# Linear attention and a SwiGLU gate on one core: every PSUM-fed query evacuation split between ScalarE and VectorE, and both denominator runs placed in gate/up

## The chip, the cores and the metric

The kernel runs on one core of a Trainium2 chip. The metric is the device time of one execution in microseconds (us); the time given for the kernel before is the median of three runs. TensorE is PE in the profile (its weight loads PEld), VectorE is DVE, ScalarE is ACT, GpSimd is POOL, and SyncE (SP) issues all DMAs.

## The reference

The inputs are bf16: x is 1 x 2048 x 1024, wqkv 1024 x 3072, wo 1024 x 1024, w_gate and w_up 1024 x 3584, w_down 3584 x 1024. A second x among the inputs is not used.

```python
def A(xn):                                     # linear attention, 32 heads of 32
    q, k, v = split(xn @ wqkv)
    phi = lambda t: where(t > 0, t + 1, exp(t)) + 1e-6
    pq, pk = phi(q), phi(k)
    kv  = einsum("bhsd,bhse->bhde", pk, v)
    z   = einsum("bhsd->bhd", pk)
    num = einsum("bhqd,bhde->bhqe", pq, kv)
    den = einsum("bhqd,bhd->bhq", pq, z)[..., None] + 1e-6
    return heads_together(num / den) @ wo
def B(xn):
    return (silu(xn @ w_gate) * (xn @ w_up)) @ w_down
xn = layernorm(x)
out = x + A(xn) * silu(B(xn))
```

## The kernel before, in words

All large products but the smallest are Strassen-Winograd products of seven multiplications (called m = 1 to 7), and some of the seven (those in a set J) are split into seven again. One such product is a *pair*: two weight blocks (w = 0, 1) against one token half of 1024 tokens (p = 0, 1). A result of 2 x 2 blocks comes out of PSUM by the callback `evac(w, i, j, ...)`, where i is the column block and j the token block. Three of the four results are read from a PSUM bank (`kind == "ps"`: from m = 2, m = 3 and m = 4), the fourth from an SBUF tile (`"sb"`, m = 7). In each pair m = 6 and m = 7 go on in the same banks, and DVE adds drain them (`step(w, m)`); a split product has four steps (`fresh(m, k)`), whose sums also run on DVE and ACT.

The stages are, in this order: layer norm, transposition and the keys and values (kv); four *query pairs* `q_pair(p, s)`, with s the half of the columns; 28 gate/up pairs `gu_pair(p, n)`; four pairs for s = (normalised queries) @ M, where M combines kv and wo; and the down projection with the final sum. Among the queries the sixteen blocks of M are made as well (`m_build`, each a small product, an ACT evacuation and a DMA store to `m_scratch`).

- `phi_evac` computes phi of a drained block. ACT makes Exp; DVE takes min(e, 1) + 1e-6 (the tensor_scalar in line 1041). Then one of two forms follows. With `relu` false, a DVE scalar_tensor_tensor makes max(t, 0) + e (line 1048) and reads t from its source, a PSUM bank where kind is "ps". With `relu` true, ACT makes Relu(t) into an SBUF tile of the pool H1 and DVE adds two SBUF tiles (line 485). `RQ` chooses the form for the queries, `RK` for the keys.
- `den_run(s)` makes the denominators of half s from the finished queries of both token halves: 32 small matmuls with Zh into one bank, one DVE tensor_scalar (line 1296), four DVE reciprocals (line 1298), an ACT copy, and eight DMAs into `r_scratch`.
- `normalise(p, j, half)` reads `r_scratch` back, scales the rows on ACT and multiplies the queries on DVE, then stores them in `q_scratch`. Eight such calls stand behind gate/up pairs z = 4, 6, ..., 18 (`N0`, `NS`); the first four are half 0.
- The sums of weights that Strassen needs (`combos`) and the sums for the split products (`inner`) run on POOL for gate/up, except the combos of its first weight block, which run on DVE.

Nothing of the order is written out by hand below the level of these calls. `Plan.op` records every operation with its reads and writes, `Plan.schedule` gives each a due time from what depends on it, and then chooses, for all engines together, the operation that can start first by its own costs; banks and buffers are given out there as well. The chosen order is what each engine runs, with semaphores between engines. So moving one call can move operations of others on every engine. Operations of DVE that read SBUF alone are marked `port`, and the planner starts them only when POOL's current operation is over by its own costs; on the chip nothing but the semaphores orders POOL against DVE.

The lines of the profile for all these are helpers: 427 for matmuls, 456 for transposes, 477 for ACT, 485 for tensor_tensor on DVE and POOL, 497 for DMAs.

## Time and profile before

| what | value |
|---|---|
| median of 3 runs | 730.34 us (730.07 to 732.97) |
| the profiled execution | 730.07 us |
| its span | 728.3 us |
| mean granted TensorE clock | 0.997 |
| PE busy | 707.5 us |
| DVE busy | 548.0 us |
| ACT busy | 365.1 us |
| POOL busy | 283.5 us |
| first denominator run, PE | at 155.22 us |
| second denominator run, PE | at 208.33 us |
| reads of `r_scratch` | 225.6 to 388.4 us |

The span is what the profile covers; the execution's own time is 1.8 us longer. The groups of the profile are named by line, engine, operation and operands; as most lines are those of helpers, an instruction is told apart by its operands (`ps` is PSUM, `SB` the large SBUF tile) and by its place in the order.

### The profile page before, as it was taken

To read this page: it belongs to the slowest core of one execution; us is meant where nothing else is said; L and a number is where in the kernel's file an instruction comes from. 1 tells how busy PE (TensorE), PEld (TensorE's weight loads), DVE (VectorE), ACT (ScalarE), POOL (GpSimd) and SP (SyncE) were. 2 spreads that over 40 slices of the span, in tenths; PEclk is the share of its full clock that TensorE was granted. 3 is DMA by queue.
4 is the path that set the end of the run, shared out by engine and by line. 5 is a ranking of instruction groups with operands and counts; after the bars stand their busy time and mean duration, and the time that the engine had idled before them with its cause. 6 is when DMAs were issued, how large, how long until landed. Compare 5 with 4: busy or idle time off the path is not lost.

```text
span 728.3 us, 11805 instructions
## 1 busy us (share of the span) xinstructions
PE 707.5 (97%) x4247; PEld 401.0 (55%) x4247; DVE 548.0 (75%) x1099; ACT 365.1 (50%) x713; POOL 283.5 (39%) x258
## 2 busy tenths in 40 slices
PE   8999999988999999999999999999999999999997
PEld 3444545544666666666666666566454455464643
DVE  6998766989997787777777777789699875555433
ACT  3777745876646556665665545445573112121212
POOL 2011000255667966788676877433640000000000
PEclk9999999999999999999999999999999999999999
DMA  9334244230234244533445824254798356473622
GB/s 297 108 82 108 45 115 147 86 119 6 84 99 131 103 150 148 167 112 121 141 156 165 264 85 137 67 167 148 255 300 259 91 157 202 132 206 90 187 73 72
DMA packets 141979, 101.58 MB, mean 139 GB/s; under 512 B 19040, under 2 KB 137056, under 8 KB 141920
## 3 DMA queue, kind: packets, MB, share of 16 engines
q1 hardware_dynamic: 141920, 100.82, 45.8%
q8 instruction: 33, 0.54, 0.3%
q14 instruction: 26, 0.21, 0.1%
HBM read 68.16 MB, written 29.49 MB: 134 GB/s over the span
## 4 chain that ended last, share of the span: by engine, by line
PE 81%; DVE 7%; DMA 7%; ACT 3%; issue 1%; SPq 0%; POOL 0%; DVEq 0%; ACTq 0%
PE ps L427 81%; DVE SB L485 3%; ACT SB L477 2%; DMA out_dram<-SB 1%; DVE SB L1041 1%; DMA SB<-q_scratch 1%; DMA SB<-in_A_x_dram 1%; DMA SB<-SB 1%; DVE SB L1048 1%; DMA SB<-h_scratch 1%; DMA SB<-in_A_wqkv_dram 1%; DVE ps L485 1%; ACT ps L477 1%; SPq L497 0%; DVE SB L1213 0%
## 5 line engine op out<-in xcount | busy, mean ns | idle before, releaser
L427 PE MATMUL ps<-SB 128*128 128x512 f16 (+4 forms) x4126 | 697.2, 331 | 12.5 <-ACT ps L477 3.3
L427 PEld LDWEIGHTS ps<-SB 128*128 128x128 f16 (+1 forms) x4126 | 395.1, 98 | 312.2 <-DVE ps L485 8.3
L485 POOL TENSOR_TENSOR SB<-SB 128x512 f16<-128x512 f16 (+5 forms) x224 | 269.4, 1238 | 190.6 <-DMA SB<-in_B_w_up_dram 75.6
L477 ACT ACTIVATE SB<-ps 128x512 f16<-128x512 f32 (+4 forms) x427 | 225.6, 559 | 178.5 <-PE ps L427 164.5
L485 DVE TENSOR_TENSOR SB<-ps,SB 128x256 f32<-128x256 f32 (+2 forms) x318 | 182.0, 592 | 71.7 <-PE ps L427 56.3
L485 DVE TENSOR_TENSOR SB<-SB 128x512 f16<-128x512 f16 (+9 forms) x316 | 184.6, 618 | 59.3 <-ACT SB L477 21.7
L485 DVE TENSOR_TENSOR ps<-ps,SB 128x512 f32<-128x512 f32 (+1 forms) x250 | 128.3, 527 | 30.3 <-PE ps L427 25.2
L477 ACT ACTIVATE ps<-ps 128x512 f32<-128x512 f32 (+1 forms) x172 | 84.2, 491 | 97.4 <-PE ps L427 93.9
L477 ACT ACTIVATE SB<-SB 128x512 f16<-128x512 f32 (+1 forms) x68 | 42.1, 620 | 78.0 <-DVE SB L485 77.5
L1005 POOL TENSOR_TENSOR rstd<-veps,neg_half 128x1 f32<-128x1 f32 x16 | 11.4, 724 | 64.2 <-DVE veps L1004 62.9
L1041 DVE TENSOR_SCALAR SB<-SB 128x512 f16<-128x512 f16 x64 | 22.7, 367 | 8.7 <-ACT SB L477 8.7
L477 ACT ACTIVATE SB<-SB,zc 128x512 bf16<-128x512 bf16 x32 | 21.9, 710 | 2.5 <-DVE SB L485 2.5
L1048 DVE SCALAR_TENSOR_TENSOR SB<-ps,SB 128x512 bf16<-128x512 f32 x25 | 16.6, 678 | 0.1
L477 ACT ACTIVATE SB<-SB,nmr,rstd 128x1024 f16<-128x1024 bf16 x12 | 14.6, 1236 | 1.2 <-DVE nmr L1007 1.1
L1001 DVE BATCH_NORM_STATS2 stats<-SB 128x6 f32<-128x512 bf16 x16 | 10.9, 683 | 3.4 <-DMA SB<-in_A_x_dram 3.4
L1048 DVE SCALAR_TENSOR_TENSOR SB<-SB 128x512 bf16<-128x512 f32 x15 | 11.3, 756 | 0.0
L1002 DVE BATCH_NORM_STATS2 stats<-SB 128x6 f32<-128x512 bf16 x16 | 10.8, 678 | 0.0
L427 PE MATMUL ps<-SB,ident 128*128 128x512 f16 x17 | 6.5, 555 | 1.4 <-POOL ident L508 1.4
L456 PE MATMUL ps<-ident,SB 128*128 128x128 f16 x40 | 3.1, 222 | 1.6 <-DVE SB L1213 1.0
L456 PEld LDWEIGHTS ps<-ident,SB 128*128 128x128 f16 x40 | 2.5, 99 | 3.9 <-DVE SB L1011 1.9
L427 PEld LDWEIGHTS ps<-SB,ident 128*128 128x128 f16 x17 | 2.1, 128 | 4.6 <-issue 2.8
L1298 DVE RECIPROCAL SB<-SB 128x64 f32<-128x64 f32 x8 | 4.4, 547 | 0.1
(28 smaller groups left out, 23.3 us busy)
## 6 DMA issues: line engine op xcount, KB each, us to landing
h_scratch<-SB SPq DMA_DIRECT2D x112, 128.0 KB, 2.9
SB<-h_scratch SPq DMA_DIRECT2D x16, 896.0 KB, 6.2
SB<-in_B_w_gate_dram SPq DMA_DIRECT2D x14, 512.0 KB, 4.2
SB<-in_B_w_up_dram SPq DMA_DIRECT2D x14, 512.0 KB, 5.4
SB<-in_B_w_down_dram SPq DMA_DIRECT2D x4, 1792.0 KB, 7.8
SB<-in_A_wqkv_dram SPq DMA_DIRECT2D x12, 512.0 KB, 7.0
SB<-in_A_x_dram SPq DMA_DIRECT2D x16, 256.0 KB, 3.1
SB<-r_scratch SPq DMA_DIRECT2D x32, 128.0 KB, 2.8
```

The lines of the kernel that those rows point to most:

```text
L427: last = h.matmul(o() if callable(o) else o, l() if callable(l) else l, r() if callable(r) else r, start=st, stop=sp, skip_group_check=True)
L456: last = h.transpose(o(), i(), ident[:, :])
L477: return op("act", reads, writes, lambda h: h.activation(ev(o), ev(i), func, **kw), n / 1200.0 + (0.055 if src == "ps" else 0.095) + (0.09 ...
L485: f = lambda h: h.tensor_tensor(ev(o), ev(a), ev(b), alu)
L1001: dve([xr] + ([named("ve", 0)] if q == 1 else []), [sA], lambda h: h.bn_stats(stats[:, j, 0, :], xa[:, 0:512]), 512)
L1002: dve([xr] + ([named("ve", 0)] if q == 1 else []), [sB], lambda h: h.bn_stats(stats[:, j, 1, :], xa[:, 512:1024]), 512)
L1005: pool([ver, nh_r], [rsr], lambda h: h.tensor_tensor(rstd[:, j, :], veps[:, j, :], neg_half[:, :], ALU.pow), 0.56)
L1041: dve([e], [e], lambda h: h.tensor_scalar(vap(e, FP16), vap(e, FP16), 1.0, EPS_PHI, ALU.min, ALU.add), 512, 3.84, urgent=PU).port = True
L1048: dve(reads + [e], [out_r], lambda h: h.scalar_tensor_tensor(out_ap, ev(src), 0.0, vap(e, FP16), ALU.max, ALU.add), 512, urgent=PU).port = ...
L1298: dve([ea], [ra], lambda h, q=q: h.reciprocal(vap(ra, F32)[:, q * 64:q * 64 + 64], vap(ea, F32)[:, q * 64:q * 64 + 64]), 400)
```

## The change

There are two parts. `RQ` becomes true for every query block that comes from PSUM, where it was true only for those with j = 1; so the blocks from m = 2 and m = 4 also take the form with Relu on ACT and an add on DVE. And the two calls of `den_run` move: the first from between the third and the fourth query pair to the third gate/up pair (z = 2), the second from z = 2 to z = 6. `ZD` is then no longer read.

```diff
     UBANK, PU = 0.0, 6.0
-    RQ = lambda w, i, j, kind: kind == "ps" and j == 1
+    RQ = lambda w, i, j, kind: kind == "ps"
     RK = lambda q, c, kind: c == 0
...
         q_pair(0, 1, Q[1], mix=mb[6:])
-        den_run(0)
         G[0] = gu_load(0)
         G[0].inner(IE, JG)
         q_pair(1, 1, Q[1])
...
             at = []
-            if z == ZD:
-                at.append(partial(den_run, 1))
+            if z in (2, 6):
+                at.append(partial(den_run, z // 6))
             gu_pair(p, n, G[n], at)
```

The function that `RQ` steers:

```python
def phi_evac(reads, src, kind, out_ap, out_r, relu=False):
    e = tmp(H1)
    act(reads, [e], partial(vap, e, FP16), src, ACT.Exp, 512, kind)
    dve([e], [e], ...min(e, 1.0) + EPS_PHI...)
    if relu:
        r = tmp(H1)
        act(reads, [r], partial(vap, r, FP16), src, ACT.Relu, 512, kind)
        tt([e, r], [out_r], ...e + r...)
        return
    dve(reads + [e], [out_r], ...max(src, 0.0) + e...)
```

In the emitted order of the changed kernel the rest moves as follows. On SP the loads of the second gate/up weights (block n = 1) come after fourteen of the sixteen block stores (before, the gate half came after ten and the up half after twelve), and the eight stores to `r_scratch` of the first run come among the h_scratch stores of gate/up. On DVE, ahead of the drain of step (w0, m7) of the last query pair stand two line-1041 instructions and two SBUF adds of `phi_evac` (before: the first denominator run's five instructions, one drain and two line-1041 instructions); seven drains from PSUM follow in a row, then eight instructions that read SBUF alone, the drain of (w0, m6) of the first gate/up pair's stretch, six more that read SBUF alone, and the drain (m5, k1). Late in gate/up the orders of the engines agree again.

## The prediction

> **What bounds the kernel now.** I read the page first, then the busy time by stretches, then PE's waits in the stretch that the change touches, then the chain and the timeline there.

> ```profile
> PE 707.5 (97%) x4247; PEld 401.0 (55%) x4247; DVE 548.0 (75%) x1099; ACT 365.1 (50%) x713; POOL 283.5 (39%) x258
> ```
> TensorE is busy for 97% of the 728.3 us span, so only its idle time and slow clock can be won. By stretches (columns: width, then busy us and instructions of PE, PEld, DVE, ACT, POOL, then granted clock, DMA share, GB/s):

> ```profile
> 124.00:153.00 29.00, 27.31 (x170) 15.25 (x168) 28.07 (x75) 23.89 (x51) 6.66 (x7) 1.00 0.33 105
> 153.00:161.00 8.00, 7.61 (x71) 4.43 (x72) 5.86 (x11) 5.09 (x12) 5.11 (x4) 1.00 0.61 187
> 161.00:182.00 21.00, 16.52 (x84) 8.34 (x83) 19.36 (x35) 12.12 (x25) 12.73 (x11) 0.92 0.02 6
> 190.00:440.00 250.00, 249.97 (x1638) 157.54 (x1637) 196.23 (x390) 143.30 (x294) 192.81 (x154) 1.00 0.43 137
> ```
> The queries (124 to 182) leave PE idle for 1.69 + 0.39 + 4.48 = 6.6 us, and 161 to 182 has a clock of 0.92. Gate/up (190 to 440) leaves 0.03 us idle. So the prize lies among the queries, and whatever moves into gate/up costs its PE time and nothing else, as long as DVE (196 of 250 us), ACT (143) and POOL (193) keep their slack. PE's waits from 124 to 190, and the timeline around the longest:

> ```profile
> PE ps L427 <- DVE SB L485: 2.9, 1, 2.9
> PE ps L427 <- DVE SB L1048: 1.1, 1, 1.1
> PE ps L427 <- DVE ps L485: 0.4, 1, 0.4
> ```
> ```profile
> 157.37 8.52 POOL L485 TENSOR_TENSOR SB<-SB 128x1024 f16<-128x1024 bf16 x4 [2.81 <-DMA SB<-in_B_w_up_dram]
> ...
> 159.80 4.04 DVE L1041 TENSOR_SCALAR SB<-SB 128x512 f16<-128x512 f16 x2
> ...
> 163.76 0.68 DVE L485 TENSOR_TENSOR SB<-ps,SB 128x512 f32<-128x512 f32 x1
> ...
> 164.49 1.03 PE L427 MATMUL ps<-SB 128*128 128x512 f16 x2 [2.91 <-DVE SB L485]
> ```
> Two L1041, usually 0.28 us each, take 4.04 us while POOL builds the combinations of the second gate/up weights, 2.13 us each (8.52 / 4). They do no more work; they wait for POOL. Behind them on DVE's queue stands the add that drains step (w0, m7) of the last query pair, and PE waits 2.91 us for it. After that PE runs 164.49 to 167.7 at half clock (the record has 3.41 us at 0.5, hence 0.92), which loses another 1.71 us. This one event costs 4.62 us.

> **The first part: sixteen evacuations.** Each query pair has four products with j = 0 drained from PSUM (m = 2 and m = 4, for w = 0 and 1); four pairs make 16. Removed are 16 L1048 with PSUM source, 0.60 us from start to start (two take 1.27). Added are 16 ACT Relu, at 0.50 (eight such evacuations take 4.03), and 16 DVE adds between SBUF tiles at 0.34 (0.41 alone, two take 0.75). DVE is relieved of 16 x 0.26 = 4.2 us, ACT gets 8.0 more.

> ```profile
> L1048 DVE SCALAR_TENSOR_TENSOR SB<-ps,SB x25: 642/677/692, 23.4 to 189.9; 128x512 bf16<-128x512 f32 x25
> L1048 DVE SCALAR_TENSOR_TENSOR SB<-SB x15: 678/681/1151, 36.2 to 194.9; 128x512 bf16<-128x512 f32 x15
> ```
> The PSUM form never exceeds 0.69 us; the form with both inputs in SBUF reaches 1.15, when POOL is at work (174.94, 175.94). An SBUF add also took 1.07 at 170.92 beside POOL's 1.14. So the new add is cheaper alone and dearer under POOL. [...]

> On ACT: from 130.91 to 153.34 it runs 45 instructions up to the copy (w0) that PE waits 0.71 us for at 153.39. In the changed order 48 stand there: four Relus and one block evacuation more, others fewer. 3 x 0.50 = 1.5 us, less the idle 0.92 at 144.70 and 0.2 at 149.06: PE goes on **0.4 us later**. If nothing absorbs it, 1.5; if earlier free banks absorb all, 0.

> **The second part: the denominators.** The first run takes from the queries 32 matmuls (1.06 us of PE), on DVE 0.42 + 2.31 us and 1.10 of idle before, on ACT 0.42, and on SP eight issues in 5.21 us.

> ```profile
> 155.22 1.06 PE L427 MATMUL ps<-SB,Zh 128*32 128x256 bf16 x32
> ...
> 156.79 2.31 DVE L1298 RECIPROCAL SB<-SB 128x64 f32<-128x64 f32 x4
> ```
> The PE time comes back whole in gate/up: net 0. There the second run stands today (PE at 208.33) without a wait of PE; the first takes that place, and the second goes four pairs on, to about 208.3 + 4 x 11.6 = 255 (eight normalisations start from 225.6 to 388.4, two pairs apart: 23.3 us per two pairs). The readers keep their places: the first half's at 225.6 stays 17 us behind, the second's at 225.6 + 4 x 23.3 = 319 is 64 us behind; a landing takes 2.8 us. On SP the eight issues no longer stand before the third gate/up weights, but among h_scratch stores; POOL has none of it. All of this I cost at 0, hidden by DVE's 54 idle us in 250; without that cover it would be its 2.7 us of DVE per run.

> **What happens at the stall.** In the changed order, four SBUF-only instructions (two L1041, two adds) stand ahead of the drain of (w0, m7), and then come seven PSUM drains in a row. PE reaches that pair at about 153.4 + 0.4; its inputs come over ACT at 0.5 us each, so the four end at about 157.3. POOL's first combination began at 157.37, after weights issued at 152.05; in the changed order those follow two to four more block stores, so not earlier. On these numbers the stall goes: **-4.6 us**. The margin is only some tenths.

> What is late next: after the seven drains come eight SBUF-only instructions (among them the adds put off), then the drain of gate/up's first (w0, m6), then six more, then the drain (m5, k1). They begin at about 164.0, with POOL in its last combination and the eight smaller inner sums still to come:

> ```profile
> 157.37 9.75 POOL L485 TENSOR_TENSOR SB<-SB 128x1024 f16<-128x1024 bf16 x5 [2.81 <-DMA SB<-in_B_w_up_dram]
> 169.77 6.77 POOL L485 TENSOR_TENSOR SB<-SB 128x256 f16<-128x256 bf16 x7 [2.65 <-PE ps L427]
> ```
> If each waits out one POOL instruction, as at 159.80 and 170.92 to 173.82, eight take 2.13 + 1.2 (9.75 - 8.52) + 6/7 x 6.77 = 9.1 us: the first drain ends at 164.0 + 9.1 + 0.7 = 173.8. PE needs it for the product (w0, m7), which it begins today at about 177.4 (its drain starts at 178.48); less 2.91, 1.71, 1.06 of waits and 1.06 of matmuls that left, plus 0.4, it is there at 171.1. It waits 2.7, then 0.9 for its product (174.7), and for the second drain (one POOL instruction 1.0, three L1041 at 0.2, two adds at 0.34, itself 0.4: 176.5) another 1.8. **New waits: 4.5 us.** Below, 0, where POOL is through early or the two alternate better; above, 8, if ACT's longer queue delays the cluster too. I take 4.5, as the rows for it are of the same instructions. The waits of 1.06 and 0.44 at 175.08 and 181.35 lie where these come, and go: **-1.5**.

> Clock: in this trace 2.91 us of idle led to half speed, 1.06 did not. 2.7 in one piece is nearer to the first, so 1.7 may be added. [...] I leave the 1.7 out of the point and keep it in the range.

> **Sum.** -4.6 - 1.5 + 0.4 + 4.5 = -1.2 us. The profiled execution took 730.07 us (span 728.3 and 1.8 around it; 0.27 below the median of 730.34): **728.9 us**. With the ends of the terms its own range is 724 (no new waits, nothing lost on ACT: -6.1) to 731.7 (1.1 more on ACT, the clock falls once).

> **Rivals.** (1) *The cluster does not bind*: the SBUF instructions slip between POOL's, or PE has other products to do, so that only 0.5 us of the 4.5 stays: -5.2, **724.9 us**. For it: DVE as a whole has 4.2 + 2.7 us less to do where it sat on the chain from 168.6 to 181.3. Against: 14 exposed instructions now, where the same stretch had eight (two at 159.80, six from 169.25 to 173.8). (2) *The old stall stays, and the new one comes*, slower: the last two of the four SBUF-only instructions are later than POOL's first combination, as ACT runs behind. It decides at 157.4: from there each costs up to 2.1 us, PE loses the 4.6 again, and the new wait brings the clock's 1.7: -1.2 + 4.6 + 1.7 = +5.1, **735.2 us**. For it: ACT was 82% busy (23.89 of 29) and gets more. Against: weights issued later. (3) *Banks*: a bank is now freed by the Relu, which stands up to 14 instructions behind its Exp (7 us), where today exp, min and L1048 span 3.6; if PE waits for banks another 2.8 us, +1.6, **731.7 us**. That the denominators stay among the queries is excluded: the emitted order has their matmuls in gate/up.

> **How the numbers follow.** Half a per cent, 3.65 us, is about what a measurement of this kernel can tell from no change. Forecast 0.40 (0.07 of it faster, 0.31 within, 0.02 slower); rival 1 0.29, all faster; rival 2 0.21, all slower; rival 3 0.10 (0.07 within, 0.03 slower). Faster 0.36, within 0.38, slower 0.26. The range, 724.0 to 734.6, leaves out the far half of rival 2 and the best of rival 1, together under 0.2.

> **What would show it.** Right: L1048 with PSUM source 9 times; no PE wait of over 1 us between 155 and 165; DVE SBUF-only instructions of 0.7 to 2.1 us in a row from about 164, and PE's longest wait after them, before gate/up's first (w0, m7); gate/up to 440 without idle PE. Wrong: PE idle under 3 us from 124 to 185 (rival 1), an L1041 or add of about 2 us before the drain of the last query pair's (w0, m7) (rival 2), PE waits on ACT (rival 3), or PE waits in gate/up around the denominators.

## The result, and the profile after

| | before | after |
|---|---|---|
| median | 730.35 us (730.07 to 732.97, 4 runs) | 742.77 us (740.08 to 743.58, 4 runs) |
| ratio, 95% interval | | 1.0156 (1.0120 to 1.0191) |
| profiled execution, its span | 730.07, 728.3 us | 740.08, 738.3 us |
| mean granted clock | 0.997 | 0.992 |

The changed kernel is slower by 12.4 us in the medians, and by 10.0 in the two profiled executions. The forecast was 728.9, and no case that it priced lay above 735.2. The other three executions show a mean granted clock of 0.989 to 0.991, so the account below covers the 10.0 of the profiled pair and not the 12.4. The busy line of the page after, then the same stretches as before and the longest waits of PE from 124 to 200 us:

```profile
PE 710.2 (96%) x4247; PEld 401.4 (54%) x4247; DVE 554.9 (75%) x1099; ACT 371.8 (50%) x729; POOL 284.3 (39%) x258
```
```profile
124.00:153.00 29.00, 25.14 (x157) 14.02 (x157) 27.34 (x69) 24.06 (x51) 8.50 (x8) 1.00 0.30 99
153.00:161.00 8.00, 8.00 (x46) 4.19 (x45) 4.47 (x12) 8.00 (x19) 0.16 (x1) 1.00 0.65 196
161.00:182.00 21.00, 15.77 (x81) 8.15 (x78) 19.16 (x27) 11.88 (x26) 16.92 (x12) 0.84 0.00 1
190.00:440.00 250.00, 244.03 (x1613) 152.58 (x1611) 197.84 (x387) 141.30 (x290) 182.73 (x144) 0.99 0.43 135
```
```profile
PE ps L427 <- ACT SB L477: 6.4, 2, 5.2
PE ps L427 <- DVE SB L485: 2.9, 1, 2.9
PE ps L427 <- DVE ps L485: 2.1, 1, 2.1
```
DVE is busy for 6.9 us more (554.9 against 548.0), though the edit should have relieved it by 4.2. PE loses time at three places and a small fourth, and its timeline has them in a row (the bracket is the idle time before the piece and who ended it):

```profile
147.39 23.69 PE L427 MATMUL ps<-SB 128*128 128x256 f16 x134 [2.06 <-DVE ps L485]
176.32 14.07 PE L427 MATMUL ps<-SB 128*128 128x256 f16 x68 [5.23 <-ACT SB L477]
191.53 1.10 PE L427 MATMUL ps<-SB 128*128 128x256 f16 x8 [1.14 <-ACT SB L477]
193.06 0.83 PE L427 MATMUL ps<-SB 128*128 128x256 f16 x6 [0.43 <-ACT ps L477]
194.11 0.61 PE L427 MATMUL ps<-SB 128*128 128x256 f16 x4 [0.22 <-ACT ps L477]
197.65 19.48 PE L427 MATMUL ps<-SB 128*128 128x256 f16 x114 [2.92 <-DVE SB L485]
...
278.88 6.46 PE L427 MATMUL ps<-SB 128*128 128x256 f16 x41 [1.25 <-DVE SB L485]
```
What POOL and DVE do there, and for the second place ACT:

```profile
139.61 7.91 POOL L485 TENSOR_TENSOR SB<-SB 128x512 f16<-128x512 f16 x7 [2.57 <-DVE SB L485]
...
142.72 4.28 DVE L485 TENSOR_TENSOR SB<-SB 128x512 bf16<-128x512 f16 x4
146.91 0.42 DVE L485 TENSOR_TENSOR ps<-ps,SB 128x256 f32<-128x256 f32 x1
...
160.84 17.23 POOL L485 TENSOR_TENSOR SB<-SB 128x1024 f16<-128x1024 bf16 x12 [13.33 <-DMA SB<-in_B_w_up_dram]
165.19 2.22 DVE L485 TENSOR_TENSOR SB<-SB 128x512 f16<-128x512 f16 x1
167.34 2.20 DVE L1041 TENSOR_SCALAR SB<-SB 128x512 f16<-128x512 f16 x1
169.46 0.41 DVE L485 TENSOR_TENSOR SB<-SB 128x512 f16<-128x512 f16 x1
169.80 1.91 DVE L1041 TENSOR_SCALAR SB<-SB 128x512 f16<-128x512 f16 x2
171.63 1.37 DVE L485 TENSOR_TENSOR SB<-SB 128x512 bf16<-128x512 f16 x1
172.92 2.71 DVE L1048 SCALAR_TENSOR_TENSOR SB<-SB 128x512 bf16<-128x512 f32 x2
173.03 1.85 ACT L477 ACTIVATE SB<-ps 128x512 f16<-128x512 f32 x4 [5.22 <-DVE SB L485]
175.55 0.69 DVE L485 TENSOR_TENSOR ps<-ps,SB 128x512 f32<-128x512 f32 x1
175.66 0.60 ACT L477 ACTIVATE SB<-ps 128x512 f16<-128x512 f32 x1 [0.78 <-DVE SB L1048]
...
190.79 6.32 POOL L485 TENSOR_TENSOR SB<-SB 128x1024 f16<-128x1024 bf16 x3 [12.71 <-DMA SB<-in_B_w_up_dram]
...
193.04 4.21 DVE L1041 TENSOR_SCALAR SB<-SB 128x512 f16<-128x512 f16 x2
```
- **142 to 147 us**: four adds, 0.41 us each when alone, take 4.28 us beside the sums for the split products of the first gate/up block. Held against the emitted order, two of them are new adds of the first query pair: their Relus stand 7.3 and 3.9 us behind their Exps on ACT (140.71 and 141.66, against 133.37 and 137.77). The third is an add of the same pair that the kernel before has too, and the fourth is one of Strassen's sums. Behind them stands the drain (m5, k1) of the third query pair, and PE waits 2.06 us.
- **165 to 176 us**: eight SBUF-only instructions in a row, as the prediction's order has them. Seven wait out one POOL instruction each; the third (169.46, 0.41 us) runs where POOL pauses for 0.08 us (169.39 to 169.47). Only one of the eight, that of 171.63, is one of the sixteen new adds. The forecast drain ends at 176.24. At the same time ACT's Exp waits 5.22 us (167.8 to 173.03) for a buffer of H1 that an add frees, and a later one 0.78 for one that the last L1048 frees at 175.63; that one empties the bank (175.66 + 0.60 = 176.26) and PE goes on at 176.32. The clock falls at 174.0, while PE still waits, and stays at half until 180.8.
- **190 to 198 us**, already in gate/up: two line-1041 instructions of the sixteen blocks, 0.28 us each when alone, take 4.21 beside the combinations of the third block. PE waits 1.14, 0.43, 0.22 and 2.92, and is at half clock from 197.91 for 3.41 us.
- **277 to 279 us**: 1.25 us more, told below.

The account of the profiled executions: PE's idle time (all bracketed pieces of the timeline added) is 22.33 us after and 14.93 before, so +7.4. Half clock costs PE half of 4.48 (176.32 to 180.8) and of 3.41, 3.95 in all, against 1.6 before (half of the 3.20 from 164.49, where PE goes on, to 167.69): +2.35. Together 9.75 of the 10.0.

The longer DVE time does not lie in the instructions that were moved. By the emitted order the sixteen new adds took 9.0 us in all, less than the 10.8 of the sixteen L1048 that they replace: thirteen took 0.41 to 0.43 us, the other three 1.37, 0.89 and 1.37. What grew are SBUF-only instructions that both kernels have, and that now run in another order beside POOL: SBUF adds other than the sixteen +5.6, line-1041 instructions +2.7, line-1048 instructions with both inputs in SBUF +0.5.

### The profile page after: what moved, and what is told of

It reads as the page before. It is cut to its first block, busy times and chain, and to the rows that moved or that the text cites. A ratio compares the mean times of both kernels' runs of the same rounds, so it can differ in the third digit from the quotient of the medians.

```text
span 738.3 us, 11825 instructions
## 1 busy us (share of the span) xinstructions
PE 710.2 (96%) x4247; PEld 401.4 (54%) x4247; DVE 554.9 (75%) x1099; ACT 371.8 (50%) x729; POOL 284.3 (39%) x258
## 4 chain that ended last, share of the span: by engine, by line
PE 81%; DVE 7%; DMA 6%; ACT 4%; issue 2%; SPq 0%; DVEq 0%; ACTq 0%
PE ps L427 81%; DVE SB L485 4%; ACT SB L477 3%; DMA out_dram<-SB 1%; DMA SB<-in_A_x_dram 1%; DMA SB<-q_scratch 1%; DMA SB<-SB 1%; DVE SB L1041 1%; DMA SB<-h_scratch 1%; ACT ps L477 1%; DVE SB L1048 1%; DVE ps L485 0%; SPq L497 0%; DVE SB L1213 0%; DVE stats L1001 0%
## 5 line engine op out<-in xcount | busy, mean ns | idle before, releaser
L427 PE MATMUL ps<-SB 128*128 128x512 f16 (+4 forms) x4126 | 699.9, 332 | 19.9 <-ACT SB L477 7.3
L427 PEld LDWEIGHTS ps<-SB 128*128 128x128 f16 (+1 forms) x4126 | 395.5, 98 | 321.8 <-ACT SB L477 13.3
L485 POOL TENSOR_TENSOR SB<-SB 128x512 f16<-128x512 f16 (+5 forms) x224 | 270.5, 1244 | 200.5 <-DMA SB<-in_B_w_up_dram 86.7
L477 ACT ACTIVATE SB<-ps 128x256 f32<-128x256 f32 (+5 forms) x443 | 233.5, 566 | 182.7 <-PE ps L427 163.4
L485 DVE TENSOR_TENSOR SB<-SB 128x512 f16<-128x512 f16 (+9 forms) x332 | 199.0, 633 | 57.6 <-ACT SB L477 20.9
L485 DVE TENSOR_TENSOR SB<-ps,SB 128x256 f32<-128x256 f32 (+2 forms) x318 | 181.7, 591 | 74.0 <-PE ps L427 58.4
L485 DVE TENSOR_TENSOR ps<-ps,SB 128x512 f32<-128x512 f32 (+1 forms) x250 | 128.0, 526 | 33.5 <-PE ps L427 27.7
L1005 POOL TENSOR_TENSOR rstd<-veps,neg_half 128x1 f32<-128x1 f32 x16 | 11.2, 711 | 64.3 <-DVE veps L1004 63.1
L1041 DVE TENSOR_SCALAR SB<-SB 128x512 f16<-128x512 f16 x64 | 25.7, 410 | 9.1 <-ACT SB L477 8.9
L1048 DVE SCALAR_TENSOR_TENSOR SB<-SB 128x512 bf16<-128x512 f32 x15 | 11.7, 790 | 0.0
L427 PE MATMUL ps<-SB,ident 128*128 128x512 f16 x17 | 6.5, 557 | 1.4 <-POOL ident L508 1.4
L1048 DVE SCALAR_TENSOR_TENSOR SB<-ps,SB 128x512 bf16<-128x512 f32 x9 | 6.0, 681 | 0.0
L427 PEld LDWEIGHTS ps<-SB,ident 128*128 128x128 f16 x17 | 2.1, 130 | 4.5 <-issue 2.8
L1298 DVE RECIPROCAL SB<-SB 128x64 f32<-128x64 f32 x8 | 4.3, 539 | 0.0
```

The lines of the kernel that those rows point to most:

```text
L427: last = h.matmul(o() if callable(o) else o, l() if callable(l) else l, r() if callable(r) else r, start=st, stop=sp, skip_group_check=True)
L477: return op("act", reads, writes, lambda h: h.activation(ev(o), ev(i), func, **kw), n / 1200.0 + (0.055 if src == "ps" else 0.095) + (0.09 ...
L485: f = lambda h: h.tensor_tensor(ev(o), ev(a), ev(b), alu)
L1005: pool([ver, nh_r], [rsr], lambda h: h.tensor_tensor(rstd[:, j, :], veps[:, j, :], neg_half[:, :], ALU.pow), 0.56)
L1041: dve([e], [e], lambda h: h.tensor_scalar(vap(e, FP16), vap(e, FP16), 1.0, EPS_PHI, ALU.min, ALU.add), 512, 3.84, urgent=PU).port = True
L1048: dve(reads + [e], [out_r], lambda h: h.scalar_tensor_tensor(out_ap, ev(src), 0.0, vap(e, FP16), ALU.max, ALU.add), 512, urgent=PU).port = ...
```

## The experiments

The theories: **P**, DVE's SBUF-only instructions wait out POOL's weight sums, and buffers and banks hand this on to ACT and PE; **D**, the later denominators give the adds later due times; **A**, ACT's 8 us of Relus more are the load that PE waits for. The kernel before ran beside all kernels, with medians of 730.2 to 731.0.

**The first part alone.**
```diff
+        den_run(0)
         G[0] = gu_load(0)
...
-            if z in (2, 6):
-                at.append(partial(den_run, z // 6))
+            if z == ZD:
+                at.append(partial(den_run, 1))
```

> The kernel before with the first part of the change alone (all sixteen blocks with Relu and an SBUF add, both denominator runs where they were). Theory P (the sixteen exposed SBUF-only instructions wait out POOL's weight sums one for one, and H1 buffers and banks hand the delay to ACT and PE): 738 to 745 us, with PE idle of over 14 us up to 240 us in the span and half-clock time of over 6 us. Theory D (the later denominators give their inputs later due times, and so the adds are put off): 728 to 732, as the denominators stand where they were. Theory A (ACT's 8 us of Relus more are what PE waits for): about 740, with the waits at ACT's instructions and not at DVE's SBUF-only ones.

Measured: 735.15 us, ratio 1.0072 (1.0047 to 1.0098): 4.9 us slower than before, less than P asked for. The waits are there, but each stays by itself:

```profile
150.65 5.15 PE L427 MATMUL ps<-SB 128*128 128x256 f16 x29 [2.14 <-DVE ps L485]
157.42 1.04 PE L427 MATMUL ps<-SB 128*128 128x512 f16 x4 [1.62 <-ACT ps L477]
...
174.83 1.47 PE L427 MATMUL ps<-SB 128*128 128x256 f16 x8 [2.06 <-ACT SB L477]
...
202.15 10.80 PE L427 MATMUL ps<-SB 128*128 128x256 f16 x70 [2.03 <-DVE SB L485]
```
Idle time is 21.67 us, nearly that of the changed kernel; but the granted clock in 120 to 240 us is 1.00 throughout, where the kernel before has its one fall. +6.7 of idle and -1.6 of clock make the 5.1 by which the spans differ (733.4 and 728.3); 2.0 of the 6.7 lie outside 138 to 450 us (0.7 ahead of it, 1.3 behind).

**The second part alone.**
```diff
-    RQ = lambda w, i, j, kind: kind == "ps"
+    RQ = lambda w, i, j, kind: kind == "ps" and j == 1
```

> The kernel before with the second part alone (denominators with gate/up pairs 2 and 6, old evacuations). Theory P: 724 to 731 us; the five DVE instructions and 1.06 us of matmuls leave the queries, no exposed instruction is added. Theory D: 738 to 743, the whole of the change's loss. Theory A: 724 to 731 as P, since ACT has nothing more to do.

Measured: 732.20 us, ratio 1.0023 (1.0004 to 1.0043). D's 738 to 743 is out; P's range is just missed. The old stall is not worth what the forecast gave for it: two other waits come, and one in gate/up.

```profile
171.53 2.41 PE L427 MATMUL ps<-SB 128*128 128x256 f16 x12 [2.09 <-ACT ps L477]
176.04 31.15 PE L427 MATMUL ps<-SB 128*128 128x256 f16 x188 [2.10 <-DVE SB L1048]
```
```profile
268.99 31.18 PE L427 MATMUL ps<-SB 128*128 128x256 f16 x202 [1.29 <-DVE SB L485]
```
The two parts add up to 4.9 + 1.9 = 6.8 of the 12.4 us; 5.6 come only when both are made.

**POOL's sums shortened, order unchanged**, in the changed kernel and then in the kernel before.
```diff
+        def few(x):
+            return x[(slice(None),) * (len(x.shape) - 1) + (slice(0, 8),)]
...
+            if eng == "pool" and isinstance(fast, str):
+                f = lambda h: h.tensor_tensor(few(o), few(a), few(b), alu)
...
+            f.few = k in (2, 3, 4)
```

> The changed kernel in the same order on every engine, but POOL's weight sums of the first three gate/up blocks are made on 8 columns of their last dimension only; the rest of these sums is left out. Theory P: the three sites lose their waits (2.06, 5.23, 2.92 us of PE and most of the 5.1 us that half clock costs): 725 to 731 us, DVE's SBUF adds and line-1041 instructions at 140 to 198 us all under 0.5 us. Theories D and A: the order and ACT's load are unchanged, so 738 to 743.

> The kernel before in its own order, with POOL's weight sums of the first three gate/up blocks made on 8 columns of their last dimension only (the rest of these sums is left out). Theory P: the old stall is POOL's as well, so its 2.91 us of idle, 1.71 us of half clock and the waits of 1.06 and 0.44 go: 724 to 727 us, and the earlier run of the changed kernel with the same cut (727.67) stays above it by the 1.3 us that it still loses in gate/up. If POOL has no part in the old stall: 729 to 731.

Measured: 727.67 us (0.9963, 0.9945 to 0.9982) for the changed kernel, so 15.1 us faster than uncut, and 724.77 (0.9913, 0.9884 to 0.9942) for the kernel before, 5.4 faster. Every instruction stands in the same order on its engine; only POOL's are short. Both runs decide for P. (Short sums are also ready earlier, but in neither kernel is a wait of PE among the queries put down to POOL itself.) In the cut changed kernel the DVE group of 165 to 176 has become this, and 161 to 182 runs at full clock with 19.85 of 21 us busy (columns as in the stretches above):

```profile
163.16 0.42 DVE L491 TENSOR_TENSOR SB<-SB 128x512 f16<-128x512 f16 x1
163.49 0.31 DVE L1047 TENSOR_SCALAR SB<-SB 128x512 f16<-128x512 f16 x1
...
164.93 1.28 DVE L1054 SCALAR_TENSOR_TENSOR SB<-SB 128x512 bf16<-128x512 f32 x2
166.13 0.69 DVE L491 TENSOR_TENSOR ps<-ps,SB 128x512 f32<-128x512 f32 x1
```
```profile
161.00:182.00 21.00, 19.85 (x115) 10.98 (x113) 16.08 (x44) 16.77 (x34) 2.93 (x11) 1.00 0.17 50
```
(The cut adds lines ahead, so line 485 is 491 here.) By the difference of the differences, 15.1 - 5.4 = 9.7 of the 12.4 us are POOL's hold during its first three blocks. The other 2.7 (2.9 by the distance of the two cut kernels) is about the idle time of PE in the cut changed kernel that is left: 1.30 us in gate/up, beside a block that the cut does not reach, and 1.15 + 0.43 + 0.22 as the queries end.

**The new Relus shortened, order unchanged.**
```diff
+                if few:
+                    op("act", reads, [r], lambda h: h.activation(vap(r, FP16)[:, 0:16], ev(src)[:, 0:16], ACT.Relu),
+                       512 / 1200.0 + 0.055)
...
+                phi_evac([v], src, kind, o, orr, RQ(w, i, j, kind), j == 0)
```

> The changed kernel in the same order on every engine, but the sixteen Relus that the change adds are made on 16 of their 512 columns; the rest of those Relus is left out. This takes about 16 x 0.4 = 6 us of work off ACT. Theory P: POOL still holds the SBUF-only adds, 736 to 743 us. Theory A: about 731 us, the added load is gone. Theory D: 738 to 743.

Measured: 741.76 us, 1.0161 (1.0126 to 1.0196). A falls: with ACT at 365.9 busy us instead of 371.8 the longest waits are much the same (5.2, 2.9 and 2.1 uncut; line 1046 is the shortened Relu).

```profile
PE ps L427 <- ACT SB L1046: 4.6, 1, 4.6
PE ps L427 <- DVE SB L485: 3.5, 1, 3.5
PE ps L427 <- DVE ps L485: 2.4, 2, 2.2
```
PE's longest wait is still put down to ACT, though ACT has less to do: ACT hands on a wait, it doesn't make it. The 1.14 at the end of the queries stays as well. There ACT loads its activation table (1.28 us, 189.58 to 190.87 in the changed kernel) behind the last evacuations and ahead of the copies that gate/up waits for. This wait has neither to do with POOL nor with the length of the Relus; why the change brings it was not settled.

**Another rule for the planner.** The planner starts an SBUF-only DVE operation no earlier than POOL is free, and lets it hold POOL off. When both could start at the same instant, DVE came first, again and again; on the chip the two took turns (in the changed kernel an add of 0.41 us took 2.22 at 165.19 beside POOL's combination of 2.12, POOL's next one began at 167.21, and the DVE instruction behind the add took 2.20). The rule gives POOL the next turn:
```diff
-                if best is None or s < best[0]:
+                if best is None or s < best[0] or (e == "pool" and s == best[0] and best[2].port and self.turn == "dve"):
...
+                if o.port or e == "pool":
+                    self.turn = e
```

> The changed kernel with one other rule in the planner: where POOL and an SBUF-only DVE operation could start at the same time and DVE had the last turn, POOL goes first, so that the plan lets the two take turns as the chip does. Theory P: the order then knows where SBUF-only operations are slow, and puts fewer ahead of the drains that PE waits for: 728 to 735, no PE wait over 3 us. If the loss does not come from the order but from the amount of exposed work: 739 to 744.

> The kernel before with the same planner rule. Theory P: the old stall at 164 us shrinks, 724 to 730. If the order does not matter: 729 to 732.

> The second part alone (denominators in gate/up, old evacuations) with the same planner rule: by theory P 724 to 730, against 732.2 without the rule; if the order does not matter, 731 to 733.

> The changed kernel with the turn rule once more, for a profile at the full clock: about 732 us. Theory P: what is left of the loss against the same rule without the sixteen (726.1) is again at SBUF-only DVE instructions beside POOL, or at banks behind them, in 138 to 200 us; if it is ACT's load, PE waits at banks that ACT drains while ACT itself is never idle.

Measured, with the same three lines in each: the changed kernel 732.06 us (1.0019, 1.0001 to 1.0036), 10.7 faster than without the rule; the kernel before 725.60 (0.9929, 0.9905 to 0.9953), 4.6 faster, and so faster than both kernels of the comparison; the second part alone 726.14 (0.9940, 0.9918 to 0.9961), 6.1 faster. The changed kernel's second run under the rule took 731.32 us and is the profile read below; its longest wait of PE is 2.38 us. Like with like, both under the rule, the changed kernel is 6.5 us over the kernel before (732.06 against 725.60), where it is 12.4 over without: the order makes about half of the loss. In the kernel before under the rule, PE's waits from 124 to 200 us are down to this:

```profile
PE ps L430 <- DVE ps L488: 1.6, 2, 1.3
PE ps L430 <- ACT ps L480: 1.6, 3, 0.7
PE ps L459 <- DVE SB L1216: 1.0, 1, 1.0
PE ps L430 <- DVE SB L488: 0.2, 1, 0.2
```
(Lines from the rule on are three higher here.) Under the rule the denominators' move costs nothing that shows (726.14 and 725.60), and the wait in gate/up is gone. The first part still costs about 6 us (732.06 and 726.14).

**The new form in some pairs only.**
```diff
-    RQ = lambda w, i, j, kind: kind == "ps"
+    RQ = lambda w, i, j, kind, s: kind == "ps" and (j == 1 or s == 0)
```

> The changed kernel with the new form only in the first two query pairs (8 of the 16 blocks); the last two keep the old form for j = 0. Denominators as in the changed kernel. Theory P: these eight adds run before POOL's first weight sums at about 139 us, so they meet nobody: 729 to 734, as the kernel with the denominators alone (732.2). If each exposed add costs the same wherever it stands: about 737.

> The mirror of the run before: the new form only in the last two query pairs, the first two keep the old form for j = 0. Theory P: nearly the whole loss, 737 to 744. If each add costs the same wherever it stands: about 737.

Measured: 737.75 us (1.0090, 1.0054 to 1.0125) with the first half's eight, 738.85 (1.0107, 1.0073 to 1.0142) with the second half's (`s == 1`). The first was a miss: eight adds of pairs that are over before POOL begins cost 5.6 us beside the kernel with the denominators alone. Three of the eight don't run where their blocks are drained. The order has the Relus of two of them late on ACT (141.36 and 142.31, their Exps at 134.02 and 138.43), and the adds behind these run at 144.18 and 145.47, beside POOL's sums; a third runs at 172.38 and takes 1.37. The other five take 0.41 each. The first two stand in this group, with an older add and one of Strassen's sums:

```profile
143.37 4.28 DVE L485 TENSOR_TENSOR SB<-SB 128x512 bf16<-128x512 f16 x4
```
This is the first place of the changed kernel once more, with the same 2.06 us of PE behind it; and PE waits 5.06 at 177.23. The sum of the halves' losses beside 732.2, 5.6 + 6.7, is more than the 10.6 of all sixteen.

**A version by form**, on the kernel before with the turn rule:
```diff
-    RQ = lambda w, i, j, kind: kind == "ps" and j == 1
+    RQ = lambda w, i, j, kind, s: kind == "ps" and s == 0
```

> A version made from the theory: the kernel before with the planner's turn rule, the form with Relu and SBUF add for all twelve or more PSUM-fed blocks of the first two query pairs (POOL idle) and for none of the last two (POOL busy), denominators as before. Theory P: 721 to 726 us, at or under the 725.6 of the rule alone. If exposure to POOL is not what counts: DVE gets 0.26 us more for each of the eight blocks that change back, and 726 to 729.

Measured: 728.23 us (0.9966, 0.9950 to 0.9983). A miss: it is slower than the rule alone. How many instructions are exposed, and in which pairs their blocks are drained, does not foretell the time.

**What is left under the rule.** The changed kernel with the turn rule and the cut of POOL's sums (both diffs above); the sixteen adds made as urgent to the planner as the operation that they replace, without and with the rule; and the same urgency for the query adds that the kernel before has already (blocks with j = 1; the adds of the keys were left as they are).
```diff
+                t = tt([e, r], [out_r], out_ap, partial(vap, e, FP16), partial(vap, r, FP16), ALU.add, 512, True)
+                if soon:
+                    t.urgent = PU
```

> The changed kernel with the turn rule (732), and POOL's weight sums of the first three gate/up blocks made on 8 columns of their last dimension only (the rest of these sums is left out). If what remains of the loss is POOL's hold on SBUF-only DVE instructions: 724 to 728, PE waits of 2.38 and 1.48 us at drains gone. If it is ACT's longer queue or the order of the drains itself: 730 to 732.

> The changed kernel, with the sixteen new adds as urgent to the planner (6 us) as the operation that they replace; nothing else. If the putting off is the cause: 728 to 735. If the strings of SBUF-only instructions ahead of a drain are the cause wherever the adds stand in them (the planned order still has strings of seven or eight): 738 to 744.

> The changed kernel with both, urgent adds and the turn rule. If both matter: 725 to 729. If the turn rule is all: 731 to 733, as without the urgency.

> The kernel before with the turn rule (725.6), and its own SBUF adds (from the blocks with j = 1 and the keys) made urgent in the same way. If putting off matters with the turn rule too: 722 to 725. If not: 725 to 727.

Measured: 728.42 us (0.9972, 0.9956 to 0.9988) with rule and cut. It is 3.6 us under the rule alone, and 2.3 over the second part alone under the rule, which was not cut; so how much of the 5.9 between those two is POOL's is not shown. PE's wait of 2.38 us goes, but that of 1.48 stays, so this half of the expectation fell. Urgent adds alone: 739.55 (1.0144, 1.0114 to 1.0173), so a low due time of the adds is not the cause by itself; strings of SBUF-only instructions stand ahead of drains there too (an add of 2.34 us at 161.86 and a line-1041 of 2.20 at 164.13, ahead of the drain for which PE waits 3.24 us). Urgent adds with the rule: 730.22 (1.0003, 0.9990 to 1.0016), 1.8 under the rule alone: between both expectations. The kernel before with rule and urgency: 727.08 (0.9961, 0.9948 to 0.9974), 1.5 over the rule alone, so there the urgency brings nothing.

## Why the prediction was wrong

The step that failed is the pricing of POOL's hold on DVE's SBUF-only instructions. The forecast knew the mechanism, but looked for it in one place, the cluster from 164 us (+4.5). It took 142 to 147 us and gate/up as free of new waits, the denominators at 0, and left the clock out of the point; so it forecast -1.2 us, and the profiled executions differ by +10.0. The runs showed 2.06 us at 147, 5.23 at 171 to 176, 4.7 and 1.7 of clock at 190 to 201, 1.25 at 278 and 2.24 of clock at 176, and with POOL's sums cut 9.7 of the 12.4 us are gone.

- **The old stall goes (-4.6): right.** It was worth 2.91 + 1.60 = 4.5; the prediction's 1.71 for the clock counts from the fall at 164.28, where PE still waits. The four SBUF-only instructions end at 159.1, POOL begins its first combination at 160.84, and the drain of (w0, m7) starts at 160.26 unhindered. POOL was later than the bound of 157.37, as the weights were. The waits of 1.06 and 0.44 (-1.5) went too.
- **ACT ahead of the copy (w0) (+0.4): wrong term.** The copy came 2.0 us later (154.63 against 152.64), and not by three instructions of ACT but by the 2.06 of PE at 147.39. The step looked for DVE beside POOL only from 164 us. The timeline before has POOL at work there; that adds come beside it could be read from the emitted order:

```profile
141.39 4.99 POOL L485 TENSOR_TENSOR SB<-SB 128x512 f16<-128x512 f16 x4 [3.77 <-DVE SB L485]
```
- **The cluster (+4.5): right in mechanism and nearly in size, wrong in its last link.** Seven of eight instructions wait out one POOL instruction each: 10.4 us (165.19 to 175.55) for the 9.1 of the estimate, from a start 1.2 later. PE's wait begins at 171.09, which meets the 171.1 worked out for (w0, m7) by luck: by the emitted order it waits there two small products earlier, (m1, k0) and (m5, k1), and would have been at (w0, m7) at about 172.0 to wait 4.3 for the drain. What it did wait for, 5.23 in one piece and not 2.7 + 1.8, was a bank: ACT was late as well, starved of H1 buffers by the same cluster; the forecast had no term for buffers. No run gives H1 more buffers, so this link rests on the rows. Rival 3 had banks freed late by the length of ACT's queue, and the cut Relus show that length didn't matter.
- **Clock (1.7, left out of the point): wrong.** Leaving it out failed twice, 2.24 us from 176.32 and 1.7 from 197.91, while the old 1.6 went.
- **Gate/up without idle: the worst step.** 1.14 + 0.43 + 0.22 + 2.92 = 4.7 us of idle and 1.7 of clock at 190 to 201, where the forecast had none. The 2.92 and the clock behind it come as two SBUF-only instructions beyond the fourteen that were counted meet the next block's combinations; the 1.14 + 0.43 + 0.22 stand at ACT's table load, and their cause is open.
- **Denominators at 0: off by 1.25.** The priced cover, DVE's idle time in gate/up, was not the one that counted. The second run's instructions (up to 269.2 us) push two multiplications of `normalise` into POOL's combinations (269.42 to 279.9), where the two take 3.24 us; PE waits. The denominators alone show much the same, 1.29. No run cuts POOL's sums there, so this rests on the rows.
- **"The new add is cheaper alone and dearer under POOL": true as a risk, small as a cost.** Three of the sixteen adds waited, 2.4 us together; the loss came by other instructions, whose place in the order changed with them.

Summed with what was measured: -4.5 - 1.5 + 2.06 + 5.23 + 2.24 + 4.7 + 1.7 + 1.25 = +11.2, and 1.1 us less idle behind 450 us and 0.4 less ahead of 138 leave 9.7 of the 10.0. All the losses but the 1.14 + 0.43 + 0.22 are the mechanism that the forecast knew and priced at one place of four. What the trace before showed against the change (line 1048 never over 0.69 us from PSUM, 1.15 with both inputs in SBUF while POOL worked) held: an SBUF add of 0.41 us alone took 2.22 beside POOL, and 0.42 with POOL's sums cut. What was missing was to follow it wherever POOL works.

Not settled: why both parts together cost 5.6 us more than each alone. In the profiled executions PE's idle time from 138 to 450 us is 5.1 before, 9.8 with the first part, 6.3 with the second and 14.0 with both; half clock costs 1.6, 0, 1.7 and 3.95. So beyond the sum of the two parts, both together cost 2.9 of idle time and 3.8 of clock; why the two orders add up so is open. Also open are the waits at ACT's table load, and what is left of the first part's loss under the turn rule (728.42 with POOL's sums cut, against 726.14 for the second part alone, uncut).

## What to carry to other kernels

An operand moved from PSUM to SBUF was here not only another duration (an add of 0.41 us in place of a line-1048 instruction of 0.68): it exposed the instruction to POOL (three of the sixteen adds took 1.37, 0.89 and 1.37), and it changed the order of the instructions around it. Only those three waited; most of the loss came by others that now stood beside POOL. So hold the whole new order of SBUF-only instructions against every stretch of POOL in the trace, not only the one under study. A planner that models a shared resource has to model who goes next at a tie; here that one rule was worth 4.6 us to the kernel before, and 10.7 to the changed one. A wait put down to ACT may be a buffer that DVE holds: shorten the suspected work in place, order unchanged, before believing it.

## What the runs showed of the hardware

DVE and POOL took turns one for one. In the changed kernel, with POOL's instructions back to back, seven of the eight SBUF-only DVE instructions from 165.19 to 175.63 each waited out one POOL instruction: they took 2.22, 2.20, 1.24, 0.75, 1.37, 1.15 and 1.63 us, against 0.28 to 0.68 for the same forms alone, beside POOL instructions of 0.71 to 2.18. POOL's next instruction began between each two of them, and DVE was not idle in between. The eighth (169.46, 0.41 us) ran where POOL had paused for 0.08 us. The waiting lies inside the DVE instructions: the rows show no idle time of DVE, for a semaphore or for anything else, ahead of the seven. So what is said ahead of the prediction, that nothing but the semaphores orders POOL against DVE, does not hold here. Not every instruction that reads SBUF alone waited: in the kernel before, the three reciprocals that start from 157.37 to 158.55, beside POOL's first combination (157.37 to 159.49), took 0.55 each, and the last in the changed kernel (268.74), with POOL idle, 0.54.
